# TensorE's order in an adaLN transformer block: a plan of time in place of a credit

## The chip, the cores and the metric

The kernel runs on one core of a Trainium2 chip. The metric is the device time of one execution in microseconds (us), as a median over several executions. Five engines matter: TensorE (PE, with its weight loads PEld), VectorE (DVE), ScalarE (ACT), GpSimd (POOL) and SyncE (SP), which here only issues DMAs.

## The reference

One transformer block in float32 over 2048 tokens of width 576. Six modulation vectors come from `c`; an attention with 32 heads of width 18 and a feed-forward layer of width 4608 with SiLU stand in two residual branches.

```python
mod = (silu(c) @ w_mod).reshape(...)            # sa, ca, ga, sb, cb, gb
h = layernorm(x) * (1 + ca) + sa
q, k, v = split(h @ wqkv)                       # 32 heads x 18
p = softmax(q @ k.T * 18 ** -0.5)
x = x + ga * ((p @ v) @ wo)
h = layernorm(x) * (1 + cb) + sb
x = x + gb * (silu(h @ w1) @ w2)
```

## The kernel before

Each float32 product that needs accuracy is made of three passes over split operands (high, low) in the fast `fp32r` type: 14 passes cover the 576 inputs of a projection (`PASS`). The product of probabilities and values is plain float32.

A prologue makes the layer norm, V for all tokens and the first Q and K. Then the attention goes over four blocks of 512 queries (`NQB`), in each over eight quads of four heads (`NQUAD`), 32 quads in all. In each quad two streams run, shifted by `LEAD` = 38 pairs of slots:

- `slot_a`: scores with queries on the partitions (`psa`), for a maximum over keys on VectorE (`mx`). `max_a` and `max_b` turn the maxima into extra rows of Q (transpose `pst`, then four DMAs on SP).
- `slot_b`: scores with keys on the partitions (`psb`); ScalarE takes the exponential into a tile `pt`. `pt` has 7 buffers (`PB`).

The two use opposite halves of TensorE's rows (54 and 56 of 64), so a `psa` and a `psb` matmul run side by side: one score pair, counted as one slot (`now`). A quad has 64 slots. `pv` adds a key tile's values into `psv`: four float32 matmuls side by side in four column groups. 16 key tiles make a quad's values; ScalarE copies them (`ov`), and `out_b` transposes them (`pso`) for division by the sums.

Between slots TensorE does filler work from a list (`Filler`): in block 0 the remaining Q and K projections (`qk_pair`), in blocks 1 to 3 the output projection (`proj`) and the feed-forward layer (`mlp1`, `mlp2`) of the block before. What is left of block 3's comes after the attention, alone, as the tail. A filler product has two PSUM banks (`Pair`), one for each half of the rows; a step is two matmuls side by side, and in the middle of a pair the halves change banks, which waits for a turn on ScalarE (`nop`). PSUM's eight banks are rings: `psb` 2, `psv` 1, and in block 0 `psF` 2 and `psA` 3; from the end of block 0 `psF` 3 and `psA` 2. The rings `psF` (fillers, `ps`, `psqk`, `psT`) and `psA` (`psa`, `pst`, `pso`) are what the change reckons with.

TensorE runs its instructions in the order in which the program writes them; those of the other engines are put in order by the build. The order of TensorE is set by the main loop: a slot, then values when due (`PVD` = 4 slots behind a second key tile, always two tiles: `PVN`), then filler steps as far as a credit allows, which grows by the same amount each slot and is charged for values (`PVC`). Nothing in it asks whether a bank is free.

Of the kernel before, what the change touches and what calls it, by code (L numbers as in the profile page):

```python
# [60 lines left out]
PVN = 2  # L61
DEBT = 1500.0
# [14 lines left out]
IDLE = 1  # L77
PVX = 300.0
PVC = 550.0
# [9 lines left out]

class Filler:  # L90


    def __init__(self):
# [7 lines left out]
    def add(self, cost, fn=None, name=None, fresh=False):  # L101

        self.items.append((cost, fn, name, fresh))
        self.total += cost

    def pace(self, slots):
        self.rate = (self.total - self.done) / max(slots, 1)
        self.credit = 0.0

    def _one(self):  # L110
        cost, fn, _, _ = self.items[self.pos]
        self.pos += 1
        self.done += cost
        if fn is not None:
            fn()
        return cost

    def step(self, extra=0.0, force=False):
        self.credit += self.rate + extra
        given = 0.0  # L120
        while self.pos < len(self.items) and not (given > 0 and self.items[self.pos][3]) and (self.credit > 0 or (force and given <= 0 and self.credit > -DEBT)):
            cost = self._one()
            self.credit -= cost
            given += cost
        return given > 0

    def until(self, name):
        last = max(i for i, it in enumerate(self.items) if it[2] and name in it[2])
        while self.pos <= last:
            self.credit -= self._one()  # L130

    def flush(self):
        while self.pos < len(self.items):
            self._one()
# [3 lines left out]
def tile_adaln_block(ctx: ExitStack, tc: tile.TileContext, x, wqkv, wo, w1, w2, c, wfirst, wcol, out):  # L138
# [70 lines left out]
    PASS = list(passes())  # L209

    class Pair:
# [6 lines left out]
        def __init__(self, ps, ops, n, halves):  # L218
            self.ps, self.ops, self.n, self.halves = ps, ops, n, halves

        def step(self, s):
# [5 lines left out]
            for h in (1, 0) if late else (0, 1):  # L227
# [4 lines left out]
                if h == 1 and s == self.n - 1:  # L232
                    self.turn = nc.scalar.nop()
                    tc.add_manual_dep(self.turn.ins, done.ins.name, SYNC, reason="the last of the first halves")
                elif h == 1 and s == self.n:
# [30 lines left out]
    def mod_piece(m, t):  # L266
# [5 lines left out]
        nc.scalar.activation((ga if m == 0 else gb)[:, t * P:t * P + n], ps[:, :n], AF.Copy)  # L272

# [22 lines left out]
    def qk_pair(which, m, ns, w, part):  # L296
# [8 lines left out]
        if part == NG - 1:  # L305
            for g in range(2):
                qk_out(which, m, ns[g], qk_ps[0].ps[g])

# [133 lines left out]
    state = {"now": 0, "k": 0, "tail": False, "tail2": False}  # L442
# [5 lines left out]
    fill = Filler()  # L448
    qk_w = {}

    def add_qk(steps):
# [5 lines left out]
        for i, (which, m, pairs) in enumerate(steps):  # L457
            for ns in pairs:
                names = [("qkx"[which], m, n) for n in ns]
                for p in range(NG):  # L460
                    fill.add(MMC * len(GR[p]), lambda i=i, which=which, m=m, ns=ns, p=p: qk_pair(which, m, ns, qk_w[i], p), name=names, fresh=p == NG // 2)
# [63 lines left out]
    later = []  # L525

    def slot_a(s, j):
# [11 lines left out]
        nc.vector.tensor_reduce(t["mx"][:, 2 * j + hp, stt, kc:kc + 1], ps, axis=AX.X, op=ALU.max)  # L539
        if j == 1 and s % 32 == 31:  # L540
            now = 2 * s + 1
            later.append((now, lambda: max_a(t)))
            later.append((now + MB, lambda: max_b(t)))

    def max_a(t):
# [5 lines left out]
        t["ms"] = ms  # L551

    def max_b(t):
# [3 lines left out]
        nc.vector.tensor_copy(mt, ps[:32, :P])  # L557
        for i in range(4):
# [3 lines left out]
    def slot_b(s, j):  # L562
# [3 lines left out]
        if j == 0:  # L566
            if w == 0:
                if i == 0:
                    fill.pace(NQUAD * 64 - END0)
                t["P"] = {}  # L570
            if w == 16 and i + 1 < NQ:
                load_v(i + 1)
            t["P"][kt, hp] = att.tile([P, 2, QB], F32, tag="p", name="pt", bufs=PB)
# [6 lines left out]
        if hp == 1 and j == 1 and kt % PVN == PVN - 1:  # L580
            later.append((state["now"] + PVD, lambda: pv(i, t, kt - PVN + 1, PVN)))

    def pv(i, t, k0, n):
        state["pv"] = True
        fill.credit -= PVC * n
        if k0 == 0:
            t["ps"] = psV.tile([P, QB], F32, tag="v", name="psv2")
        for kt in range(k0, k0 + n):
# [4 lines left out]
        if k0 + n == NKT:  # L593
            ov = att.tile([P, QB], F32, name="ov", bufs=1)
            nc.scalar.activation(ov, t["ps"], AF.Copy)
            later.append((state["now"] + 2, lambda: out_b(i, ov)))

    def out_b(i, ov):
# [11 lines left out]
        for s4 in range(NST):  # L610
            nc.vector.tensor_mul(o[b][:, s4, 72 * qd:72 * qd + 72].rearrange("p (h c) -> p h c", h=4), psr[:, s4, :, :DH],
                                 rec[:, s4, :, None].to_broadcast([P, 4, DH]))
        del quads[i]
# [5 lines left out]
    def open_mlp():  # L619
# [6 lines left out]
        mp["p"] = ctx.enter_context(tc.tile_pool(name="mlp", bufs=1, side="right"))  # L626

# [33 lines left out]
    def post(b):  # L661
# [3 lines left out]
        fl.__init__()  # L665
        ob = o[b]
        c = ready[b]
        last = state["tail"] = b == NQB - 1

        def o_T(kt):  # L670
# [6 lines left out]
            hi = c["th"][:, kt, :]  # L677
            nc.scalar.activation(hi, ps, AF.Copy)
# [5 lines left out]
        def proj(j, part):  # L684
# [8 lines left out]
            if part == len(GP) - 1:  # L693
                for g in range(2):
                    add_x1(j, g, c["pp"].ps[g])

# [9 lines left out]
        def ln_a(j):  # L706
            mv = pool.tile([P, 1, 2], F32, name="mv2", bufs=4)
            ln_stats(pool, c["x1"][j], mv[:, 0, :])
            c["ln", j] = mv, ln_rstd(pool, mv, 1)
# [5 lines left out]
        def h_T(kt):  # L715
# [3 lines left out]
            ps = bank("psT", psF)  # L719
            for j in range(NST):  # L720
# [7 lines left out]
        for kt in range(KT):  # L728
            fl.add(600, lambda kt=kt: o_T(kt))
        if b == 0:  # L730
            fl.add(LP0)
        for j in range(NST):
            rest(4 if j < 3 else 0)
            for part in range(len(GP)):
                fl.add(MMH * 7, lambda j=j, part=part: proj(j, part), fresh=part == 2)
                if part == 2 and j:
# [4 lines left out]
        rest(3)  # L741
# [27 lines left out]
        def mlp1(i, part):  # L769
# [11 lines left out]
            if not state["tail"]:  # L781
# [3 lines left out]
                nc.vector.tensor_copy(us[1], c["p1"].ps[1])  # L785
            for g_ in range(2):
# [8 lines left out]
        def mlp2(i0, j, part):  # L795
# [10 lines left out]
            for hf in range(2):  # L806
                add_x1(j, hf, c["p2"].ps[hf])
            if i0 + CH == NFT:
                nc.sync.dma_start(out[b * QB + j * P:b * QB + (j + 1) * P, :], c["x1"][j])

        if not EARLY:
            for kt in range(KT):
                fl.add(1100, lambda kt=kt: h_T(kt), name=["h_T"])
# [3 lines left out]
        if EARLY:  # L817
            if b == 0:
                fl.add(LP)
            for kt in range(KT):  # L820
                fl.add(1100, lambda kt=kt: h_T(kt), name=["h_T"])

        def add_mlp1(i, w2n=()):

            for part in range(NG):
                fl.add(MMC * len(GR[part]), lambda part=part: mlp1(i, part), fresh=part == NG // 2)
# [7 lines left out]
        def add_mlp2(i0, add):  # L834
            for j in range(NST):
                for part in range(len(G2)):
                    add(MMH * len(G2[part]), lambda j=j, part=part: mlp2(i0, j, part), None, part == 2)
# [12 lines left out]
        else:  # L850
            fl.add(0, lambda: prefetch(b + 1))
            add_mlp2(NFT - CH, lambda *a: left.append(a))
            fl.pace(NQUAD * 64 - END)

    def run_later(now):
        nonlocal later
        due = [e for e in later if e[0] <= now]
        later = [e for e in later if e[0] > now]
        for e in due:
            e[1]()  # L860
# [9 lines left out]

    fill.rate = V_RATE
    fill.step(WARM)
    fill.credit = 0.0
    idle = 0
    for now in range(2 * (total + LEAD + 8)):
        state["now"] = now
        state["pv"] = False
        sa, j = divmod(now, 2)
# [3 lines left out]
        if sa < LEAD:  # L882

            if j == 0:
                slot_a(sa, 0)
                slot_a(sa, 1)
        elif sa < total:
            slot_a(sa, j)
        if now >= ON0 and now % ONS == 0 and (now - ON0) // ONS < 2 * NKB:
            ones_rows(*divmod((now - ON0) // ONS, 2))  # L890
        if 0 <= sa - LEAD < total:
            slot_b(sa - LEAD, j)
        run_later(now)
        if sa < LEAD:
            fill.step()
        else:
            p0 = state["pv"]
            if p0:
                fill.credit += fill.rate + PVC / 4
                if fill.credit > PVX:  # L900
                    fill.step(-fill.rate)
                idle = 0
            elif fill.step(PVC / 4, idle >= IDLE):
# [53 lines left out]
```

## Time and profile before

| | |
|---|---|
| median of 3 runs | 2694.21 us (2691.33 to 2695.09) |
| the profiled execution | 2698.32 us, span 2696.5 us |
| mean granted TensorE clock | 0.972 |
| PE / DVE / ACT / POOL busy | 93% / 66% / 55% / 22% |
| scores' maxima on DVE (L539) | 2048 x 687 ns |
| exponentials on ACT (L579) | 2048 x 597 ns |

The span is the time from the first to the last instruction of the profiled execution. An engine's busy share is over the whole span. In a row of waits stand the engine and line that waited, who ended it, the sum in us, the count and the longest. In a timeline row stand the start, the length, engine, line, operation, tiles out<-in, shapes and count; in brackets the idle time before it and who ended that.

### The profile page before, as it was taken

The numbers are of one execution on the slowest core, as the hardware profiler recorded it, in microseconds if no ns is written. First come the engines' busy times: TensorE is split into PE (matmuls) and PEld (weight loads), VectorE is DVE, ScalarE is ACT, GpSimd is POOL, SyncE is SP. The second block draws the span as 40 slices with busy tenths as digits, with TensorE's granted clock in tenths as the row PEclk, the third lists the DMA queues.
The fourth block names the chain that finished last, engine by engine and source line by source line (L and its number), as shares of the span: only waits on it lengthen the run. The fifth ranks groups of instructions, "written<-read, shape, count | busy, mean of one in ns | idle before, by whom it ended". The sixth has DMA issues, their size and how long they took to land.

```text
span 2696.5 us, 51333 instructions
## 1 busy us (share of the span) xinstructions
PE 2505.7 (93%) x20248; PEld 1657.0 (61%) x20248; DVE 1771.5 (66%) x3097; ACT 1483.4 (55%) x2696; POOL 600.6 (22%) x827
## 2 busy tenths in 40 slices
PE   6969999998899999999899999999899999999999
PEld 5845444442456666666566666666566666658998
DVE  8367787776776777776776777666777676514333
ACT  2205676665565666666566666665666666661211
POOL 4200000002356556563211111111211111111000
PEclk8979999997999999999999999999999999999999
DMA  7452323324245545554433333333433333324653
GB/s 241 155 191 83 112 82 98 101 76 160 90 157 173 172 154 170 180 164 149 146 107 119 137 126 119 137 115 108 163 128 120 137 118 105 112 95 175 220 193 129
DMA packets 155042, 372.03 MB, mean 138 GB/s; under 512 B 17498, under 2 KB 50682, under 8 KB 154802
## 3 DMA queue, kind: packets, MB, share of 16 engines
q1 hardware_dynamic: 154658, 368.45, 40.2%
q8 instruction: 161, 2.64, 0.4%
q14 instruction: 79, 0.65, 0.1%
q10 hardware_dynamic: 144, 0.29, 0.1%
HBM read 282.35 MB, written 85.80 MB: 137 GB/s over the span
## 4 chain that ended last, share of the span: by engine, by line
PE 75%; DVE 15%; ACT 4%; issue 3%; DMA 2%; POOL 1%; SPq 0%; ACTq 0%; DVEq 0%; POOLq 0%
PE ps L231 22%; PE psv L591 17%; PE psa L537 12%; PE ps L225 9%; DVE mx L539 8%; PE psb L577 7%; PE psqk L231 3%; DVE etmp L789 2%; ACT pt L579 2%; PE psv L391 2%; PE psp L231 1%; DVE x L700 1%; ACT etmp L788 1%; ACT etmp L784 1%; PE psp L225 1%
## 5 line engine op out<-in xcount | busy, mean ns | idle before, releaser
L539 DVE TENSOR_REDUCE mx<-psa 128x1 f32<-128x512 f32 x2048 | 1345.0, 687 | 571.9 <-PE psb L577 286.9
L579 ACT ACTIVATE pt<-psb 128x512 f32<-128x512 f32 x2048 | 1171.9, 597 | 739.1 <-PE psb L577 416.3
L577 PE MATMUL psb<-qt,kt 56*128 56x512 f32 x2048 | 846.2, 441 | 17.0 <-ACT pt L579 13.3
L537 PE MATMUL psa<-kt,qt 54*128 54x512 f32 x2048 | 797.5, 427 | 53.8 <-DVE mx L539 33.1
L537 PEld LDWEIGHTS psa<-kt,qt 54*128 54x128 f32 x2048 | 365.8, 189 | 375.4 <-issue 164.7
L591 PE MATMUL psv<-pt,vt 128*32 128x512 f32 x4096 | 516.9, 624 | 0.0
L231 PE MATMUL ps<-w2t,g 64*128 64x288 f32 x4992 | 449.8, 300 | 23.0 <-DVE x L700 13.1
L231 PEld LDWEIGHTS ps<-w2t,g 64*128 64x128 f32 x4992 | 394.0, 187 | 75.3 <-DVE x L700 33.4
L231 PE MATMUL ps<-hh,w1t 64*128 64x512 f32 x2160 | 412.6, 402 | 11.3 <-ACT etmp L784 8.8
L577 PEld LDWEIGHTS psb<-qt,kt 56*128 56x128 f32 x2048 | 362.1, 187 | 84.0 <-ACT pt L579 65.5
L231 PEld LDWEIGHTS ps<-hh,w1t 64*128 64x128 f32 x2160 | 229.0, 186 | 72.5 <-ACT etmp L784 13.1
L591 PEld LDWEIGHTS psv<-pt,vt 128*32 128x32 f32 x4096 | 109.9, 112 | 244.7 <-issue 244.2
L792 POOL TENSOR_TENSOR g<-etmp,g 128x512 fp32r<-128x512 f32 x108 | 141.0, 1321 | 492.0 <-ACT g L791 381.7
L704 POOL TENSOR_TENSOR x<-x,gt 128x288 f32<-128x288 f32 x116 | 93.3, 804 | 487.0 <-ACT gt L703 463.7
L231 PE MATMUL ps<-hl,w1t 64*128 64x512 f32 x864 | 191.3, 393 | 0.0
L700 DVE TENSOR_TENSOR x<-ps,x 128x288 f32<-128x288 f32 x184 | 83.9, 456 | 113.6 <-PE ps L225 75.4
L225 PE MATMUL ps<-w2t,g 128*128 128x288 f32 x960 | 132.2, 297 | 3.3 <-ACT g L791 1.7
L225 PEld LDWEIGHTS ps<-w2t,g 128*128 128x128 f32 x960 | 129.9, 190 | 5.2 <-ACT g L791 2.2
L231 PE MATMUL psqk<-hTh,wqh 64*128 64x512 f32 x300 | 98.5, 433 | 22.8 <-DVE qkhl L312 22.2
L231 PEld LDWEIGHTS ps<-hl,w1t 64*128 64x128 f32 x864 | 98.5, 186 | 15.3 <-issue 0.3
L280 POOL TENSOR_TENSOR wql<-raw,wqh 128x640 fp32r<-128x640 f32 x13 | 20.7, 1591 | 389.5 <-ACT wqh L279 188.3
L225 PE MATMUL ps<-hh,w1t 128*128 128x512 f32 x360 | 106.9, 390 | 0.5 <-DVE hh L199 0.5
(127 smaller groups left out, 2125.4 us busy)
## 6 DMA issues: line engine op xcount, KB each, us to landing
w1t<-w1s SPq DMA_DIRECT2D x108, 640.0 KB
w2t<-w2s SPq DMA_DIRECT2D x108, 576.0 KB
kt<-kscr SPq DMA_DIRECT2D x512, 108.0 KB
w1s<-w1t SPq DMA_DIRECT2D x36, 640.0 KB
w2s<-w2t SPq DMA_DIRECT2D x36, 576.0 KB
vt<-vscr SPq DMA_DIRECT2D x32, 608.0 KB
qt<-qscr SPq DMA_DIRECT2D x128, 108.0 KB
raw<-in_w SPq DMA_DIRECT2D x72, 160.0 KB
```

Of the source, the lines that this page charges most:

```text
L225: mm(self.ps[late], lhsT=lhsT, rhs=rhs, start=(i == 0), stop=(i == self.n - 1))
L231: done = mm(self.ps[g], lhsT=lhsT[rows], rhs=rhs[rows], start=(s == 0), stop=(s == 2 * self.n - 1))
L391: mm(ps[:, :HH], lhsT=act[:, kt, ts], rhs=wv[kt][:, b, hf * HH:(hf + 1) * HH], start=(i == 0), stop=(i == 13))
L537: mm(ps, lhsT=t["q"][64 * j:64 * j + 54, hp, stt * P:(stt + 1) * P], rhs=t["k", kc, hp][64 * j:64 * j + 54, :], start=True, stop=True)
L539: nc.vector.tensor_reduce(t["mx"][:, 2 * j + hp, stt, kc:kc + 1], ps, axis=AX.X, op=ALU.max)
L577: mm(ps, lhsT=t["k", kt // 4, hp][64 * e:64 * e + 56, kt % 4 * P:(kt % 4 + 1) * P], rhs=t["q"][64 * e:64 * e + 56, hp, :], start=True, sto ...
L579: nc.scalar.activation(t["P"][kt, hp][:, e, :], ps, AF.Exp, scale=SCALE)
L591: mm(t["ps"][32 * h:32 * h + 32, :], lhsT=t["v"][:, c0:c0 + 32], rhs=t["P"][kt, h // 2][:, h % 2, :], start=(kt == 0), stop=(kt == NKT - 1 ...
L700: nc.vector.tensor_add(c["x1"][j][:, hs], ps, c["x1"][j][:, hs])
L704: nc.gpsimd.tensor_add(c["x1"][j][:, hs], c["x1"][j][:, hs], t)
L789: nc.vector.scalar_tensor_tensor(t, t, 1.0, u, op0=ALU.add, op1=ALU.mult)
L792: (nc.vector if last else nc.gpsimd).tensor_tensor(g[:, 1, :], t, f(g[:, 0, :]), op=ALU.subtract)
```

## The change

The credit is replaced by `Plan`, which keeps a clock `t` of TensorE, a queue for ScalarE and VectorE with a price for each evacuation, and for each ring of banks the times at which its banks come free. While the program is written, the main loop asks it before each decision whether the next thing could start at once: a score pair needs a free `psa` and `psb` bank and a free `pt`; a filler pair two banks (`pair_need`), its middle the turn (`half_need`); values need their exponentials. It takes what is ready, steered by how far the slots stand ahead of the filler (`AHEAD`). Values go in runs of one to three key tiles as they are ready. Filler steps are cut finer (`G2`, `GP`). Nothing of it runs on the chip: only the order of the instructions changes. In the last block's tail the plan is off.

```diff
-PVN = 2
-DEBT = 1500.0
-G2 = [range(i, i + 6) for i in range(0, 24, 6)]
-GP = [range(i, i + 7) for i in range(0, 28, 7)]
+G2 = [range(i, i + 3) for i in range(0, 24, 3)]
+GP = [range(i, i + 2) for i in range(0, 28, 2)]
+TS, TV, TX, TL, TR = 231, 906, 290, 430, 60
+TMAX, TEXP = 690, 600
+AHEAD = 12
+LOADED = 900
+STAND = 0
+class Plan:
...
+    def op(self, eng, ready, dur, done=None):
+        self.n += 1
+        heapq.heappush(self.queue[eng], (ready, self.n, dur, done))
...
+    def when(self, name, n=1):
+        size, rel = self.rings[name]
+        ts = [0]
+        for i in range(len(rel), len(rel) + n):
+            if i >= size:
+                if i - size >= len(rel) or rel[i - size] is None:
+                    return None
+                ts.append(rel[i - size])
+        return max(ts)
...
+    def is_ready(self, when):
+        return self.off or when is not None and when <= self.t
...
 class Filler:
-    def step(self, extra=0.0, force=False):
-        self.credit += self.rate + extra
...
+    def target(self):
+        return self.span[0] + self.span[1] * self.done / max(self.total, 1.0)
...
+    def ready(self):
+        need = self.items[self.pos][3]
+        return need is None or self.plan.is_ready(need())
...
+    def pair_need():
+        return plan.when("f", 2)
...
-        if hp == 1 and j == 1 and kt % PVN == PVN - 1:
-            later.append((state["now"] + PVD, lambda: pv(i, t, kt - PVN + 1, PVN)))
+        plan.op("A", plan.t + TL - TS + 30, TEXP, done)
+        if hp == 1 and j == 1:
+            pend.append((i, t, kt, at))
...
+    def run_pv(n):
+        i, t, kt, _ = pend[0]
+        plan.t += TX + TV * n
+        pv(i, t, kt, n)
+        del pend[:n]
...
-    for now in range(2 * (total + LEAD + 8)):
...
+        n = kts_ready()
+        room = state["p"] + (now % 2 == 0) <= PB
+        scores = more and room and plan.is_ready(plan.when("b")) and (now // 2 >= total or plan.is_ready(plan.when("a")))
+        busy = work and fill.ready()
+        if n >= 3 or n and more and not room and (ahead < 0 or not busy):
+            do = "v"
+        elif not mp:
+            if scores and ahead < AHEAD:
+                do = "s"
+            elif n and plan.backlog("V") >= LOADED * n:
+                do = "v"
+            elif busy and ahead > -AHEAD:
+                do = "f"
...
+        elif busy and ahead >= 0:
+            do = "f"
+        elif n >= 2 and not busy:
+            do = "v"
+        elif scores and ahead < AHEAD:
+            do = "s"
+        elif busy and ahead > -AHEAD:
+            do = "f"
+        elif n >= 2 or n and stood >= STAND:
+            do = "v"
```

(`mp` is empty in block 0.) Three places show how the order of TensorE moves. In the rows `psa` and `psb` together are a score pair, `psv` values (`x4` is one key tile), `psqk` a step of a Q or K projection, `ps<-w2t,g` half a step of the second layer, `pso` the out transposes.

TensorE in block 0, quad 3, before: around a run of values.

```order
L231 MATMUL psqk<-hTh,wqh 128x512 x2
L231 MATMUL psqk<-hTh,wql 128x512 x2
L537 MATMUL psa<-kt_1243,qt 128x512
L577 MATMUL psb<-qt,kt_1248 128x512
L591 MATMUL psv_3971<-pt,vt_1250 32x512 x8
L537 MATMUL psa<-kt_1244,qt 128x512
L577 MATMUL psb<-qt,kt_1247 128x512
L537 MATMUL psa<-kt_1244,qt 128x512
L577 MATMUL psb<-qt,kt_1247 128x512
L537 MATMUL psa<-kt_1244,qt 128x512
L577 MATMUL psb<-qt,kt_1248 128x512
```

The same quad after:

```order
L655 MATMUL psa<-kt_1243,qt 128x512
L697 MATMUL psb<-qt,kt_1247 128x512
L655 MATMUL psa<-kt_1243,qt 128x512
L697 MATMUL psb<-qt,kt_1247 128x512
L734 MATMUL psv_3980<-pt,vt_1250 32x512 x4
L655 MATMUL psa<-kt_1243,qt 128x512
L697 MATMUL psb<-qt,kt_1248 128x512
L655 MATMUL psa<-kt_1243,qt 128x512
L697 MATMUL psb<-qt,kt_1248 128x512
L344 MATMUL psqk<-hTh,wqh 128x512 x2
L344 MATMUL psqk<-hTh,wql 128x512 x2
```

Two key tiles in one run became one tile every four score pairs, and three pairs in a row became two.

TensorE in block 2, quad 18, before: where one pair of the second layer ends and the next begins.

```order
L231 MATMUL ps_19194<-w2t,g 128x288
L231 MATMUL ps_19195<-w2t,g 128x288
L537 MATMUL psa<-kt_1247,qt 128x512
L577 MATMUL psb<-qt,kt_1237 128x512
L231 MATMUL ps_19306<-w2t,g 128x288
L231 MATMUL ps_19307<-w2t,g 128x288
```

After:

```order
L344 MATMUL ps_19208<-w2t,g 128x288
L344 MATMUL ps_19209<-w2t,g 128x288
L734 MATMUL psv_18877<-pt,vt_1250 32x512 x4
L655 MATMUL psa<-kt_1247,qt 128x512
L697 MATMUL psb<-qt,kt_1238 128x512
L655 MATMUL psa<-kt_1247,qt 128x512
L697 MATMUL psb<-qt,kt_1238 128x512
L344 MATMUL ps_19327<-w2t,g 128x288
L344 MATMUL ps_19328<-w2t,g 128x288
```

Between the two pairs there now stand a key tile of values and two score pairs instead of one score pair.

TensorE at the out transposes of quad 19, before and then after:

```order
L537 MATMUL psa<-kt_1237,qt 128x512
L577 MATMUL psb<-qt,kt_1241 128x512
L602 MATMUL pso<-ident,ov 128x128 x4
L231 MATMUL ps_19703<-hl,w1t 128x512
L231 MATMUL ps_19704<-hl,w1t 128x512
```

```order
L344 MATMUL ps_20761<-w2t,g 128x288
L344 MATMUL ps_20762<-w2t,g 128x288
L747 MATMUL pso<-ident,ov 128x128 x4
L734 MATMUL psv_20806<-pt,vt_1250 32x512 x8
L655 MATMUL psa<-kt_1245,qt 128x512
L697 MATMUL psb<-qt,kt_1236 128x512
```

They moved from behind a score pair, whose maximum frees the bank they need, to behind filler steps.

More of the change, by code (lines that the diff above doesn't have):

```diff
@@ L852, in post @@
             add_mlp2(NFT - CH, lambda *a: left.append(a))
[L853 to L860, printed above, removed]
+            fl.pace(state["now"], NQUAD * 64 - END)
     total = NQ * 32
@@ L881, in tile_adaln_block @@
             prefetch(0)
[L882 to L891, printed above, removed]
-            slot_b(sa - LEAD, j)
[L893 to L903, printed above, removed]
-                idle = 0
-            else:
-                idle += 1
+        state["now"] = now
```

254 lines of the change are left out of this document (209 added, 45 removed).

## The prediction

> **What bounds the kernel now.** I read the page first, then the span cut into blocks, then the places where TensorE waits, then single moments.
>
> ```profile
> span 2696.5 us, 51333 instructions
> PE 2505.7 (93%) x20248; PEld 1657.0 (61%) x20248; DVE 1771.5 (66%) x3097; ACT 1483.4 (55%) x2696; POOL 600.6 (22%) x827
> PE 75%; DVE 15%; ACT 4%; issue 3%; DMA 2%; POOL 1%; SPq 0%; ACTq 0%; DVEq 0%; POOLq 0%
> ```
>
> TensorE carries 75% of the chain that ended last, VectorE 15%. But 93% busy is not 93% at pace, since ends are modelled. So I price TensorE's work from start to start and look for what is left over. The stretches are cut at the copy of a quad's values (L595); columns are length, PE, PEld, DVE, ACT, POOL busy, granted clock, DMA share, GB/s.
>
> ```profile
> 272.50:608.20 335.70, 316.57 (x2044) 161.15 (x2044) 258.26 (x464) 227.81 (x423) 7.73 (x5) 0.97 0.30 94
> 608.20:677.10 68.90, 59.82 (x263) 18.88 (x265) 43.66 (x74) 37.74 (x65) 19.14 (x30) 0.73 0.48 155
> 677.10:1257.60 580.50, 545.02 (x4882) 350.99 (x4883) 417.14 (x697) 359.30 (x651) 323.33 (x464) 0.98 0.48 157
> 1257.60:1841.20 583.60, 553.89 (x5090) 363.15 (x5092) 411.30 (x704) 361.74 (x661) 92.68 (x110) 0.99 0.37 128
> 1841.20:2418.00 576.80, 546.16 (x5003) 355.62 (x5003) 358.25 (x620) 358.38 (x656) 92.80 (x110) 0.99 0.34 120
> ```
>
> These are quads 1 to 6 of block 0, its quad 7, and blocks 1, 2, 3 (580.5 + 583.6 + 576.8 = 1740.9 us). What lies ahead of 272.5 and behind 2418.0 keeps its order nearly. No engine but PE is over 77% in any of them.
>
> Paces, from one stretch of block 2:
>
> ```profile
> 1502.64 0.39 PE L537 MATMUL psa<-kt,qt 54*128 54x512 f32 x1
> ...
> 1505.92 0.40 PE L577 MATMUL psb<-qt,kt 56*128 56x512 f32 x1
> 1506.24 1.92 PE L591 MATMUL psv<-pt,vt 128*32 128x512 f32 x16
> 1506.70 0.13 PEld L591 LDWEIGHTS psv<-pt,vt 128*32 128x32 f32 x4 [0.30 <-issue]
> 1507.13 0.13 PEld L591 LDWEIGHTS psv<-pt,vt 128*32 128x32 f32 x4 [0.30 <-issue]
> 1508.10 0.50 PE L537 MATMUL psa<-kt,qt 54*128 54x512 f32 x1
> 1508.44 0.63 PE L231 MATMUL ps<-hh,w1t 64*128 64x512 f32 x4
> 1508.63 0.69 DVE L539 TENSOR_REDUCE mx<-psa 128x1 f32<-128x512 f32 x1 [1.60 <-PE psb L577]
> 1508.67 0.60 ACT L579 ACTIVATE pt<-psb 128x512 f32<-128x512 f32 x1 [1.69 <-PE psb L577]
> ...
> 1510.82 1.09 PE L231 MATMUL ps<-w2t,g 64*128 64x288 f32 x12
> 1511.62 0.40 PE L577 MATMUL psb<-qt,kt 56*128 56x512 f32 x1
> ```
>
> From 1502.64 to 1505.92 stand 14 units (a score pair or a step of two 512-column halves): 3.28 / 14 = 0.234 us each. Six steps of 288 columns take 1511.62 - 1510.82 = 0.80, so 0.133. A run of two key tiles of values goes by groups 0.43 apart, two to a tile, so 0.86 a tile. Around it: entry 0.32 instead of 0.234 (+0.09), 1508.10 - 1506.24 = 1.86 instead of 1.72 (+0.14), and the next unit 0.34 instead of 0.234 (+0.11). So each run, however long, costs 0.34 us beside its tiles. During it VectorE idles 1.60 and ScalarE 1.69 us.
>
> **Ledger of blocks 1 to 3**, by the counts in the order before: 1454 score pairs, 76 lone score halves and 1504 steps at 0.234 = 710.0; 2832 steps at 0.133 = 376.7; 384 value tiles at 0.86 = 330.2; 192 runs at 0.34 = 65.3; some 50 for transposes, which both orders share (an estimate). Sum 1532. So 1740.9 - 1532 = 209 us are waits and lost pace. Where they are, over these blocks:
>
> ```profile
> PE psa L537 <- DVE mx L539: 26.1, 47, 1.4
> PE ps L231 <- ACT etmp L784: 18.5, 39, 0.9
> PE ps L231 <- DVE x L700: 15.3, 62, 0.4
> PE pso L602 <- DVE mx L539: 13.7, 21, 1.3
> PE psb L577 <- DMA qt<-mt: 3.3, 1, 3.3
> PEld psa L537 <- DVE mx L539: 101.6, 165, 1.7
> PEld ps L231 <- DVE x L700: 42.2, 80, 0.8
> PEld ps L231 <- ACT etmp L784: 28.8, 33, 1.2
> PEld ps L231 <- ACTq L233: 22.4, 87, 0.5
> PEld pso L602 <- ACT pt L579: 19.8, 20, 1.7
> ```
>
> All but the one on a DMA are waits for a bank: a score's (psa), a filler pair's (ps; the ACTq rows are the turn between its halves), the out transposes' (pso). The PE rows are lower bounds, since a matmul's modelled end (0.40) lies past the next start (0.234); the PEld rows are upper ones. Filler pairs: between 33.8 and 93.4, taken at 85, near the upper end, because a held weight load holds its matmul. Scores: 26.1 to 101.6, taken at 60, the middle, because loads run ahead of scores. Out transposes and the maxima's: 13.7 to 33.5, taken at 23. The other 41 is lost pace, half clock included.
>
> **The change, part by part.** Both orders hold the same 18,190 matmuls; DVE, ACT, POOL and the DMAs do the same work. Only order moves.
>
> *Shorter runs of values.* The order before has 256 runs, all of two tiles. After there are 455: 128 in block 0, 327 in blocks 1 to 3. That is 135 more there, x 0.34 = +46 us of TensorE time, with nothing beside it to hide it. In block 0 it is 72 more, 24 us, laid where PE waits anyhow, so in its cycle below. The Trainium skill (TensorEngine Tiling (Array Packing), Key Properties) says that a change of tiling mode drains TensorE, which speaks against this part; this trace agrees with a cost, 0.34 us, and by the rule alone 199 runs would be 68 us lost.
>
> *Filler pairs.* Before, 59 of 72 second-layer pairs that follow one another start less than 1 us of TensorE work behind the last (median: one score pair, 0.23), while the evacuation takes:
>
> ```profile
> L700 DVE TENSOR_TENSOR x<-ps,x 128x288 f32<-128x288 f32 x104 | 47.2, 454 | 36.9 <-PE ps L231 21.2 <-PE psb L577 9.6
> L784 ACT ACTIVATE etmp<-ps 128x512 f32<-128x512 f32 x53 | 31.6, 595 | 9.7 <-PE ps L231 9.6
> ```
>
> Three banks serve pairs of two, so the second bank is always one just left. After, 5 of 72 start so early; the median stands 1.66 us behind, a value run and score pairs between, and the half-turns likewise. 0.454 or 0.595 plus some 0.5 until the result is there (1508.10 to 1508.63) fits in 1.66 even behind one maximum of 0.69. So 85 falls to 8: -77. What is late next is the maximum behind a crowded VectorE, below.
>
> *Scores.* Adjacent score pairs fall from 286 to 211, three in a row from 18 to 4. With two psa banks and 0.69 + 0.5 from score to free bank, the third in a row always waits; spaced ones wait when VectorE is behind with additions and copies. It is 72% busy in block 1, so some stay: 60 falls to 23, -37. Both ends: 0 and -60.
>
> *Out transposes.* 22 of 24 stood right behind a score and waited for its maximum; now 21 of 24 stand behind filler steps: 23 to 6, -17. The maxima's transpose and the four SP transfers behind it (L560) may come two slots later (a slot is one score pair); at least seven slots of 1740.9 / 1530 = 1.14 us stay before the first exponential needs them, some 8 us, which hide them. If that cover failed, the price is a wait like the one of 3.3 us on `qt<-mt` above, at most once a quad.
>
> *Block 0.* Here a score waits for ScalarE and its two banks:
>
> ```profile
> PEld psb L577 <- ACT pt L579: 51.1, 136, 1.1
> 419.86 0.49 PE L537 MATMUL psa<-kt,qt 54*128 54x512 f32 x1
> 426.53 0.49 PE L537 MATMUL psa<-kt,qt 54*128 54x512 f32 x1
> ```
>
> From behind one run of two to behind the next (eight score pairs) 6.67 us pass. After, a cycle of four pairs reads S S steps S S run: by the rows above the third pair can start 0.57 + 0.60 behind the first, the fourth 0.60 later, and the run with its pair takes 0.234 + 0.86 + 0.34 = 1.43, so 1.17 + 0.60 + 1.43 = 3.20, or 6.40 for eight. That is -0.27 x 8 cycles x 6 quads = -13; if ScalarE is never late, VectorE's four maxima with their side work (258.26 busy of 335.70) are the floor, -77 at most; 0 if drift eats it. I take -18, near the worked cycle. Quad 7 runs at a granted clock of 0.73, which costs up to 0.27 x 68.9 = 18.6; shorter gaps should give back half, -9. The Trainium skill (TensorE: Matmul & The Clock Gate, Part 1) says the clock halves after an idle window of about 3.4 us; by it all 18.6 would come back if no such window stays, and the trace agrees only so far that the low clock stands where PE has least work. 30 filler steps moved into quad 0: 30 x 0.234 = 7, half hidden, +3.
>
> **Sum.** -77 - 37 - 17 + 46 - 18 - 9 + 3 = -109. The profiled execution took 2698.3, 4.1 over the median of 2694.2: 2698.3 - 109 = 2589, less 4, 2585.
>
> **Rivals.** (A) *The switches cost more than the waits, slower.* 85 us over 170 pair starts and as many half-turns is 0.25 a place, less than the 0.34 that now covers it. If filler waits are only the 33.8 of the PE rows, scores keep theirs, and in block 0 PE becomes the bound (+24): -34 - 17 + 46 + 24 = +19, 2713; up to +68. It decides where less than 46 of the 209 go. Against it: starts of less than 1 us are nearly gone. 0.13. (B) *VectorE takes the waits over*: maxima stand behind the additions, and a third of 168 goes: -56 + 46 - 24 = -34, 2660. Speaks for it: 15% of the chain. 0.15. (C) *All 209 go*: -209 + 46 - 24 = -187, 2507. 0.15. (D) *Nothing comes of it*, since the engines' own queues are ordered apart from TensorE's and stand behind each other anew: within 0.2%, about what a measurement here can tell. 0.05.
>
> **How the numbers follow.** The forecast has 0.52 (own range 2540 to 2630). Faster: 0.52 + 0.15 + 0.15 = 0.82; same 0.05; slower 0.13. From 2500 (C, and a little of its tail left out) to 2690 (B and D in, A out) stands 0.82.
>
> **What would show it.** Right: filler waits on etmp and x near nothing; the out transposes' wait for maxima gone; blocks 1 to 3 at 535 to 555 us each; about 450 runs of values with 0.34 around each; VectorE's idle behind a run about 0.8, not 1.60. Wrong: psa waits on mx over 80 us in PE rows (B), blocks over 580 with filler waits gone (A), block 0 unmoved with ScalarE still the releaser.

## The result and the profile after

The changed kernel takes 2561.6 us (median of 4 runs, 2560.43 to 2563.05) against 2694.65 for the kernel before on the same chip: a ratio of 0.9505 [0.9489, 0.9522], 133 us less. 2585 was forecast, so it gained more than it was to, by some 23 us. The profiled execution took 2563.05 us.

The page of the changed kernel: span, busy times, and who carries the chain that ended last.

```profile
span 2561.2 us, 51319 instructions
PE 2448.4 (96%) x20248; PEld 1630.9 (64%) x20248; DVE 1773.2 (69%) x3097; ACT 1489.4 (58%) x2696; POOL 603.9 (24%) x827
PE 85%; DVE 7%; DMA 3%; ACT 2%; POOL 2%; issue 1%; SPq 0%; ACTq 0%; DVEq 0%
```

Against the same lines of before: as many matmuls on the same tiles, TensorE at 85% of the chain (was 75%), VectorE at 7% (was 15%). So less of the chain runs over VectorE; which waits of TensorE went is seen below.

The span of the changed kernel cut at the same events as before: quad 0 and what is ahead of it, quads 1 to 6 of block 0, quad 7, then blocks 1, 2 and 3, and the tail (start:end, length, busy time and count of PE, PEld, DVE, ACT and POOL, granted clock, DMA share, GB/s).

```profile
0.00:288.80 288.80, 222.68 (x1392) 165.70 (x1394) 175.52 (x342) 84.90 (x154) 54.91 (x75) 0.91 0.49 162
288.80:609.20 320.40, 314.73 (x1980) 148.12 (x1982) 258.75 (x460) 225.08 (x420) 7.77 (x5) 0.99 0.31 93
609.20:665.50 56.30, 46.22 (x269) 16.07 (x271) 42.95 (x74) 37.09 (x67) 19.14 (x30) 1.00 0.60 192
665.50:1217.70 552.20, 537.00 (x4914) 348.74 (x4914) 420.08 (x706) 366.52 (x662) 322.88 (x464) 0.99 0.51 167
1217.70:1746.90 529.20, 526.11 (x5018) 352.30 (x5020) 407.59 (x697) 359.07 (x652) 93.23 (x110) 1.00 0.40 135
1746.90:2284.30 537.40, 533.96 (x5037) 356.16 (x5039) 360.52 (x622) 362.90 (x659) 92.80 (x111) 1.00 0.39 132
2284.30:2561.20 276.90, 267.70 (x1648) 243.85 (x1648) 107.83 (x197) 53.80 (x88) 13.20 (x33) 1.00 0.51 179
```

| us | before | after | change | forecast |
|---|---|---|---|---|
| up to the end of quad 0 | 272.5 | 288.8 | +16.3 | +3 |
| quads 1 to 6 | 335.7 | 320.4 | -15.3 | -18 |
| quad 7 | 68.9 | 56.3 | -12.6 | -9 |
| block 1 | 580.5 | 552.2 | -28.3 | |
| block 2 | 583.6 | 529.2 | -54.4 | |
| block 3 | 576.8 | 537.4 | -39.4 | |
| blocks 1 to 3 | 1740.9 | 1618.8 | -122.1 | -85 |
| tail | 278.5 | 276.9 | -1.6 | 0 |

Two differences stand out: blocks 1 to 3 gained 37 us more than forecast, and the start lost 16.3 where 3 had been allowed. They partly cancel in the total.

TensorE's waits in blocks 1 to 3 of the changed kernel, the window 665.5 to 2284.3 (engine and line that waited, who ended it: sum in us, count, longest):

```profile
PE psa L655 <- DVE mx L657: 7.5, 15, 1.7
...
PE pso L747 <- ACT pt L699: 1.2, 1, 1.2
PE pso L747 <- DVE mx L657: 0.6, 1, 0.6
...
PEld psa L655 <- DVE mx L657: 105.6, 145, 1.9
...
PEld ps L344 <- ACTq L346: 7.3, 9, 0.8
...
PEld ps L344 <- DVE x L851: 1.7, 4, 0.8
```

The filler pairs' waits for their evacuations, 33.8 us in the PE rows and 93.4 in the PEld rows before, are gone but for some 9. So is the out transposes' wait for maxima (13.7, now 0.6). Scores' waits for their bank fell from 26.1 to 7.5 in the PE row, while the PEld row stayed where it was (101.6, now 105.6). What that row holds is seen in the timeline of weight loads, here in block 2:

```profile
1507.88 0.16 PEld L734 LDWEIGHTS psv<-pt,vt 128*32 128x32 f32 x8 [0.16 <-issue]
1508.88 0.18 PEld L655 LDWEIGHTS psa<-kt,qt 54*128 54x128 f32 x1 [0.84 <-DVE mx L657]
1508.88 0.29 PEld L697 LDWEIGHTS psb<-qt,kt 56*128 56x128 f32 x2
```

The first load behind a run of values stands idle 0.84 us (the median before and after) while the values are worked off, whatever releaser is named. That is no wait for a bank, and it lies in the 0.86 of a tile and the 0.34 of a run already. Of the 145 in the row after, some 100 with 85 us are of this kind; of the 165 before, 31 with 26. So I sum the idle ahead of every weight load of blocks 1 to 3 but the values' own, whatever its releaser, and leave out the first load behind a run of values. What remains is called held loads below; it is worked out from the timelines of blocks 1 to 3, where idle time of 0.15 us or more is told.

Values in block 0 of the changed kernel, from the timelines of VectorE and TensorE (start, length, work; in brackets the idle time before it):

```profile
421.04 2.48 DVE L657 TENSOR_REDUCE mx<-psa 128x1 f32<-128x512 f32 x4 [0.74 <-PE psa L655]
...
424.17 2.48 DVE L657 TENSOR_REDUCE mx<-psa 128x1 f32<-128x512 f32 x4 [0.65 <-PE psa L655]
...
427.31 2.48 DVE L657 TENSOR_REDUCE mx<-psa 128x1 f32<-128x512 f32 x4 [0.65 <-PE psa L655]
```

```profile
422.64 1.07 PE L734 MATMUL psv<-pt,vt 128*32 128x512 f32 x8
...
423.63 0.50 PE L655 MATMUL psa<-kt,qt 54*128 54x512 f32 x1
...
423.97 0.40 PE L655 MATMUL psa<-kt,qt 54*128 54x512 f32 x1
```

Four maxima come every 3.13 us (3.20 was worked out), and VectorE idles 0.65 behind a run (0.8 was). A run of one tile costs what a run of two does beside its tiles: from its start to the next score 0.99 = 0.86 + 0.13, and the unit behind that score takes 0.34 instead of 0.234. (The x8 counts matmul records, two to each of the four matmuls.)

### The profile page after: what moved, and what is told of

Read it like the earlier page. It is cut to its first block, busy times and chain, and to the rows that moved or that the text cites. A ratio compares the mean times of both kernels' runs of the same rounds, so it can differ in the third digit from the quotient of the medians.

```text
span 2561.2 us, 51319 instructions
## 1 busy us (share of the span) xinstructions
PE 2448.4 (96%) x20248; PEld 1630.9 (64%) x20248; DVE 1773.2 (69%) x3097; ACT 1489.4 (58%) x2696; POOL 603.9 (24%) x827
## 4 chain that ended last, share of the span: by engine, by line
PE 85%; DVE 7%; DMA 3%; ACT 2%; POOL 2%; issue 1%; SPq 0%; ACTq 0%; DVEq 0%
PE ps L344 26%; PE psv L734 19%; PE psa L655 14%; PE ps L338 9%; PE psb L697 9%; DVE mx L657 3%; PE psqk L344 3%; PE psv L508 2%; PE psp L344 2%; DMA kt<-kscr 1%; ACT pt L699 1%; PE pso L747 1%; PE psp L338 1%; DVE st L257 0%; DVE qkhl L429 0%
## 5 line engine op out<-in xcount | busy, mean ns | idle before, releaser
L697 PE MATMUL psb<-qt,kt 56*128 56x512 f32 x2048 | 825.9, 430 | 7.6 <-ACT pt L699 5.5
L655 PE MATMUL psa<-kt,qt 54*128 54x512 f32 x2048 | 803.3, 422 | 20.3 <-DVE mx L657 16.3
L734 PE MATMUL psv<-pt,vt 128*32 128x512 f32 x4096 | 543.2, 605 | 0.0
L344 PEld LDWEIGHTS ps<-w2t,g 64*128 64x128 f32 x4992 | 403.8, 186 | 70.4 <-issue 36.6
L697 PEld LDWEIGHTS psb<-qt,kt 56*128 56x128 f32 x2048 | 355.3, 184 | 68.5 <-ACT pt L699 58.1
L344 PE MATMUL ps<-hh,w1t 64*128 64x512 f32 x2160 | 381.3, 395 | 0.7 <-POOL hh L287 0.6
L344 PEld LDWEIGHTS ps<-hh,w1t 64*128 64x128 f32 x2160 | 218.0, 186 | 58.1 <-issue 16.8
L734 PEld LDWEIGHTS psv<-pt,vt 128*32 128x32 f32 x4096 | 90.9, 108 | 154.7 <-issue 148.0
L344 PE MATMUL ps<-hl,w1t 64*128 64x512 f32 x864 | 182.6, 393 | 1.3 <-POOL hl L285 1.3
L344 PE MATMUL psqk<-hTh,wqh 64*128 64x512 f32 x300 | 84.7, 428 | 35.5 <-DVE qkhl L429 34.8
L943 ACT ACTIVATE eq<-ps 128x512 f32<-128x512 f32 x36 | 21.5, 599 | 146.3 <-PE ps L338 146.3
```

What stands on the lines that cost most here:

```text
L344: done = mm(self.ps[g], lhsT=lhsT[rows], rhs=rhs[rows], start=(s == 0), stop=(s == 2 * self.n - 1))
L655: mm(ps, lhsT=t["q"][64 * j:64 * j + 54, hp, stt * P:(stt + 1) * P], rhs=t["k", kc, hp][64 * j:64 * j + 54, :], start=True, stop=True)
L697: mm(ps, lhsT=t["k", kt // 4, hp][64 * e:64 * e + 56, kt % 4 * P:(kt % 4 + 1) * P], rhs=t["q"][64 * e:64 * e + 56, hp, :], start=True, sto ...
L734: mm(t["ps"][32 * h:32 * h + 32, :], lhsT=t["v"][:, c0:c0 + 32], rhs=t["P"][kt, h // 2][:, h % 2, :], start=(kt == 0), stop=(kt == NKT - 1 ...
```

## The experiments

Three things had to be explained: what of the gain is the plan's asking for free banks (**banks**), what is the shorter runs of values (**short runs**), and why the start lost. The forecast had held banks to be nearly everything, and short runs a cost of 46 us. All ratios are to the kernel before, run beside each on the same chip.

### The start: a smaller head for quad 0

The list of projections has a credit of `WARM` ns ahead of the first slot. Before, `step` stopped after 14 of its steps, in the middle of the first pair, where the halves change banks (a step marked `fresh`); the changed `step` has no such stop, and 52 steps run ahead.

```diff
-WARM = 12000.0
+WARM = 3200.0
```

> The changed kernel with 14 instead of 52 filler steps ahead of the first score (WARM 3200 instead of 12000). Theory of the late start: quad 0 ended 16.3 us later because 38 steps (38 x 0.234 = 8.9 us, with their own bank waits) went ahead of the first maxima, in a block that VectorE and ScalarE bound. It expects quad 0 to end 9 to 14 us sooner and some of it to be kept: 2549 to 2555 us. Rival: the steps are only moved, and TensorE pays for them later: 2559 to 2563 us.

Measured: 2539.53 us, 0.9423 [0.941, 0.9435], some 22 us less than the changed kernel and better than both ranges. Quad 0 ends at 264.0 us instead of 288.8. What had gone wrong there is in two views of the changed kernel, the waits between 140 and 230 us and ScalarE's timeline:

```profile
PE psqk L344 <- DVE qkhl L429: 32.1, 8, 15.5
...
ACT wqh L395 <- DMA raw<-in_wqkv: 26.7, 1, 26.7
```

```profile
154.38 0.60 ACT L428 ACTIVATE qkhl<-psqk 128x512 fp32r<-128x512 f32 x1 [8.08 <-DMA kscr<-qkhl]
...
181.65 0.74 ACT L395 ACTIVATE wqh<-raw 128x640 fp32r<-128x640 f32 x1 [26.68 <-DMA raw<-in_wqkv]
182.29 1.07 ACT L428 ACTIVATE qkhl<-psqk 128x512 fp32r<-128x512 f32 x2
```

ScalarE's cast of the next weights (L395) waits 26.68 us for their DMA, and the copies that empty the projections' banks (L428) stand behind it in ScalarE's queue. TensorE, 38 steps further than before, has both banks full and waits up to 15.5 us. With the smaller head the first of these rows reads:

```profile
PE psqk L344 <- DVE qkhl L429: 9.9, 6, 3.8
```

That is 22.2 us less of this wait, and quad 0 ends 24.8 us sooner.

### Banks asked for, but runs of two

```diff
-        n = kts_ready()
+        n = 2 if kts_ready() >= 2 else 0
```

> The changed kernel with values always in runs of two key tiles (256 runs instead of 455), all else planned. Theory of the banks (the gain comes from laying values and score pairs where TensorE would wait for a bank; a run's switch is a loss of 0.34 us): 199 x 0.34 = 68 us less work on TensorE, of which 46 in blocks 1 to 3, against covers that are missing at a part of the pair starts (40 of 72 second-layer starts stand within 1 us again), 25 to 45 us: 2540 to 2562 us. Theory of the short runs (the gain comes from VectorE and ScalarE idling less behind a short run): most of the 122 us of blocks 1 to 3 come back, 2640 us or more.

Measured: 2613.48 us, 0.9696 [0.9683, 0.971], with 256 runs as before. Both missed: it lies 52 us above the changed kernel and 81 below the one before. The two parts of its span, quads 1 to 7 of block 0 and blocks 1 to 3:

```profile
290.70:700.50 409.80, 382.92 (x2247) 177.62 (x2249) 299.76 (x534) 265.54 (x485) 26.86 (x35) 0.93 0.31 99
700.50:2334.70 1634.20, 1590.67 (x14967) 1085.36 (x14969) 1183.40 (x2024) 1084.25 (x1971) 504.66 (x684) 0.99 0.43 144
```

Block 0 is no better than before (404.6); blocks 1 to 3 keep 107 of their 122 us.

### The old credit with runs of one

In the kernel before:

```diff
-PVN = 2
+PVN = 1
```

> The kernel before with values in runs of one tile (512 instead of 256), its credit order else unchanged. Theory of the banks: 256 x 0.34 = 87 us more work on TensorE and no wait covered on purpose; some fall under waits that were there anyhow: slower than before, 2720 to 2780 us. Theory of the short runs: faster than before by 60 us or more, 2635 us or less.

Measured: 2659.87 us, 0.9863 [0.9847, 0.9878], 1.4% less than before with 512 runs, twice as many. Both ranges missed again.

```profile
266.60:651.10 384.50, 369.20 (x2321) 170.41 (x2323) 305.00 (x537) 264.40 (x488) 26.93 (x35) 0.97 0.35 110
651.10:2382.30 1731.20, 1662.43 (x14969) 1028.76 (x14971) 1200.24 (x2021) 1094.63 (x1967) 510.49 (x684) 1.00 0.40 136
```

So neither theory held alone. Before, after and these two make a square (profiled executions, us):

| order, runs of values | block 0, quads 1 to 7 | blocks 1 to 3 |
|---|---|---|
| credit, twos (before) | 404.6 | 1740.9 |
| credit, ones | 384.5 | 1731.2 |
| plan, twos | 409.8 | 1634.2 |
| plan, mostly ones (after) | 376.7 | 1618.8 |

The new theory read off it: in block 0 the gain is the length of the runs (-20 under the credit, -33 under the plan), and the plan by itself gives little (+5 and -8). In blocks 1 to 3 it is the plan (-107 and -112), and shorter runs no more than repay what they cost (-10 and -15).

### The plan, not asking for the fillers' banks

```diff
-need={0: pair_need, len(G2) // 2: half_need}.get(part)
+need=None
```

(the same for the projections and the first layer)

> The changed kernel whose filler steps no longer ask for their banks or the turn; scores and values are still planned. 343 runs of values (230 of one tile, 57 of two, 56 of three). Theory of the banks: the waits of filler pairs come back, 75 to 100 us, less 112 runs x 0.34 = 38: 2595 to 2625 us, with PEld rows on x and etmp at 70 us or more. Theory of the short runs: most runs stay short, no more than 15 us are lost: 2550 to 2577 us.

Measured: 2677.3 us, 0.9931 [0.9918, 0.9945], far beyond both ranges. Block 0 stays (379.3); blocks 1 to 3 take 1738.2, nearly as before:

```profile
669.60:2407.80 1738.20, 1645.19 (x14993) 1087.12 (x14993) 1190.71 (x2027) 1090.12 (x1975) 508.86 (x685) 1.00 0.41 136
```

The waits in that window are back where the forecast had seen them:

```profile
PE ps L344 <- DVE x L851: 35.3, 86, 1.0
...
PE ps L344 <- ACT etmp L937: 20.1, 42, 0.9
...
PEld ps L344 <- DVE x L851: 67.5, 95, 1.2
PEld ps L344 <- ACTq L346: 40.3, 133, 0.9
PEld ps L344 <- ACT etmp L937: 31.2, 36, 1.3
```

Held loads of filler pairs are 167.7 us, where the changed kernel has 9.1. The order also has 112 runs of values fewer, worth 38 us at 0.34, so the loss of 119.4 stands for some 157 of waits, and the fillers' own 158.6 more account for it. (The plan's clock does not count these waits here, so scores and values are planned on a clock that is behind; the held loads of `psa` rose by only 10.) Asking before a filler pair carries blocks 1 to 3. The finer filler steps (`G2`, `GP`) are not the gain: this order has them too.

### Runs of two only behind block 0

The kernel with the small head, and in blocks 1 to 3 a second tile waited for:

```diff
         n = kts_ready()
+        if mp:
+            n = min(n, 1) if pend and pend[0][2] % 2 else 2 if n >= 2 else 0
```

> The kernel with the early start (WARM 3200) and runs of two key tiles in blocks 1 to 3 alone; block 0 keeps its runs of one. New theory (length matters by place: in block 0, where VectorE and ScalarE bind, short runs are worth some 33 us; in blocks 1 to 3 the 0.34 us of each further run and the score waits that it saves nearly cancel): block 0 as with the early start (378 us for quads 1 to 7), blocks 1 to 3 together 10 to 20 us longer than its 1617: 2549 to 2560 us. Rival (all of what runs of two lost, 52 us, comes back with them wherever they are): 2575 us or more. A gain would say that the switches are the greater cost.

Measured: 2563.49 us, 0.9506 [0.9485, 0.9528], against 0.9423 with the small head alone. The new theory's range was missed by a little, the other's by more. Blocks 1 to 3 lost 22.7 us (1639.5 against 1616.8), 135 runs fewer (-46 at 0.34) and 69.7 us more of held loads (134.0 against 64.3), which makes +24. Quad 7, where the edit sets in early, lost 7.3 more.

### The turn in the middle of a pair not asked for

```diff
-need={0: pair_need, len(G2) // 2: half_need}.get(part)
+need={0: pair_need}.get(part)
```

> The changed kernel whose filler pairs still ask for two free banks at their start, but not for the turn in their middle. 360 runs of values instead of 455. Theory of the banks with the start as the costly place: a turn waits some 0.25 us at 170 places, 42 us, against 95 runs x 0.34 = 32 us saved: 2562 to 2585 us. If the turn were as costly as the start (half of the 119 us that blocks 1 to 3 lost without both): 2610 us or more. Theory that the switches are the greater cost: 2550 us or less.

Measured: 2557.34 us, 0.9491 [0.9473, 0.951], between the ranges and not to be told from the changed kernel. The turn's wait is back in blocks 1 to 3:

```profile
PEld ps L344 <- ACTq L346: 44.1, 138, 0.6
```

It was 7.3, and held loads in all rose from 65.6 to 112.8. But there are 95 runs of values fewer in these blocks, 32 us at 0.34, and the blocks took only 4.4 more: what covers the turn costs about what the turn did in this order (the last run below says otherwise for another).

### Transposes at their due time

The plan also lets the out transposes and the maxima's wait until what they need is there. Here they stand at their due time:

```diff
             if cost:
-                plan.wait(when)
-                plan.wait(lambda: plan.when("a"))
                 plan.t += cost
...
-        run_later()
+        run_later(True)
```

> The changed kernel in which the transposes of the maxima and of the values go out when due, whether or not their bank and input are ready by the plan. Theory of the banks: their waits (23 us by the ledger of before, of which 17 were forecast to go) come back: 2572 to 2585 us. Rival (they are covered by TensorE's distance to their inputs anyhow): 2558 to 2566 us.

Measured: 2574.86 us, 0.9554 [0.9537, 0.9571], as expected; blocks 1 to 3 took 15.4 us more. The forecast's -17 for this step is about right. The waits in these blocks:

```profile
PE pso L747 <- DVE mx L657: 8.5, 17, 0.9
PE pst L675 <- DVE mx L657: 7.1, 10, 1.5
```

### How far the slots may run ahead

With the small head:

```diff
-AHEAD = 12
+AHEAD = 24
```

> The kernel with the early start and twice the leash between slots and filler (AHEAD 24 instead of 12), tried for a better time. If what is left (12 us in block 2, 9 in block 3, 36 in block 1 over the paced work) comes from steps that had to go by the leash although something else was ready: 2525 to 2535 us. If it comes from the start of block 1, where no filler is there yet: within 5 us of the early start, 2535 to 2545 us.

Measured: 2533.43 us, 0.9399 [0.9383, 0.9416], the lowest of all, though its interval just overlaps that of the small head alone. The total is in the first range. By the one profiled execution of each, quads 1 to 6 took 4.2 us less than with the small head alone and block 1 4.5 less, blocks 2 and 3 did not move, and quad 7 took 3.8 more. Then twice as far again:

```diff
-AHEAD = 12
+AHEAD = 48
```

> Early start with AHEAD 48. If AHEAD 24 gained 6 us because the leash forbade ready work, and block 1's start is what is left: 2522 to 2534 us. If more leash only moves filler out of quad 7, where it runs out (60.4 us with 24, 56.6 with 12): 2534 to 2545 us.

Measured: 2541.87 us, 0.9424 [0.9412, 0.9437], no better than 12 and in the second range. But the loss is in quads 1 to 6 (325.3 against 317.4), not in quad 7, which took 2.9 less than with 24.

Last, the lowest so far without the turn:

> The best so far (early start, AHEAD 24) whose filler pairs ask for their banks at the start but not for the turn in the middle: 343 runs of values instead of 451. If the turn's cover costs about what the turn's wait does, as the run without the turn said (4 us faster than the changed kernel): 2524 to 2534 us. If runs of two and three bring back score waits as in blocks 1 to 3 with runs of two (15 to 23 us): 2540 to 2555 us.

(The small head, `AHEAD` 24 and the turn not asked for.) Measured: 2564.05 us, 0.9514 [0.9501, 0.9527], worse than either range. Blocks 1 to 3 took 1648.8 us, 35.8 more than with the turn asked for: 107 runs fewer (-36), and held loads up by 69 (135.6 against 66.7), 45 of it fillers and some 20 `psa`. In the first order without the turn the fillers' had risen as much (+42) and those of `psa` by 11.5. Why scores suffer more in this order, and so whether asking for the turn pays, stays open.

### One account for all of them

Blocks 1 to 3 of nine kernels: runs of values there, held loads by kind in us, their length, and what is left of the length without 0.34 a run and without held loads. Of the scores the first kind has `psa` alone; `psb` stands with the transposes (`psT`, `pso`, `pst`), with 9.2 us before and 8.4 after.

| | runs | `psa` | filler pairs | `psb`, transposes | sum | length | left |
|---|---|---|---|---|---|---|---|
| before | 192 | 86.5 | 106.4 | 53.0 | 246.0 | 1740.9 | 1429.6 |
| credit, ones | 384 | 52.4 | 93.6 | 34.2 | 180.1 | 1731.2 | 1420.5 |
| after | 327 | 24.5 | 9.1 | 32.0 | 65.6 | 1618.8 | 1442.1 |
| plan, twos | 192 | 62.7 | 28.7 | 39.4 | 130.9 | 1634.2 | 1438.0 |
| fillers not asking | 215 | 34.7 | 167.7 | 22.3 | 224.7 | 1738.2 | 1440.4 |
| small head, late twos | 192 | 61.1 | 28.6 | 44.4 | 134.0 | 1639.5 | 1440.2 |
| turn not asked for | 232 | 36.0 | 50.9 | 25.9 | 112.8 | 1623.2 | 1431.5 |
| transposes when due | 323 | 24.6 | 13.1 | 49.4 | 87.1 | 1634.2 | 1437.3 |
| small head, `AHEAD` 24, no turn | 217 | 45.3 | 53.8 | 36.5 | 135.6 | 1648.8 | 1439.4 |

The lengths differ by 122 us, what is left by 22. So two things, the number of runs at 0.34 and the held loads, account for nearly all that these orders do to blocks 1 to 3. (What is left lies 25 to 46 us below the forecast's price of the work without runs, 1532 - 65 = 1467. So held loads say somewhat too much; that part of them hides behind matmuls that still run is likely, but not shown.)

## Why the prediction was right, and where not

**Blocks 1 to 3, the mechanism.** Waits for banks were the loss, and a plan that asks before each pair takes them away: shown by the two orders with runs of two (1740.9 to 1634.2, -106.7 at the same 192 runs) and by its undoing (+119.4 where fillers don't ask). The wait rows that were to fall fell. Rival B fell with them: the scores' wait for maxima is 7.5 us in the PE row, where 80 were its mark. Rival A too, whose blocks would have been over 580, and D, which would have left the waits as they were. C came nearest after the forecast: 171 of its 209 went.

**Blocks 1 to 3, the size.** By the forecast's own prices, with the counts of the changed kernel: 1533 score pairs and lone halves and 1512 steps at 0.234, 2832 at 0.133, 384 tiles at 0.86, 327 runs at 0.34 and 50 make 1580.6. Of 1618.8 us 38 are left as waits and lost pace; it was 209. So 171 went where 131 were forecast, and the +46 for 135 more runs came as costed. The held loads say where:

| us | forecast | held loads, before to after |
|---|---|---|
| filler pairs | -77 | 106.4 to 9.1: -97 |
| scores (held loads: `psa`) | -37 | 86.5 to 24.5: -62 |
| transposes (held loads: with `psb`) | -17 | 53.0 to 32.0: -21 |
| sum | -131 | -180 (the ledger: -171) |

The mis-sized steps are "60 falls to 23" first, then "85 falls to 8", and with them "The other 41 is lost pace", of which most was waits. (By held loads, which say somewhat too much.) The scores ended where they were forecast to, at 24.5, but began at 86.5: 60 was taken as the middle of a PE row and a PEld row, and the PEld row leaves out loads whose wait bears another releaser's name and counts the values' own time in. The fillers' 85 lies below their 106.4 for a like reason: the rows cited leave out the waits under other names and those of the output projection (`psp`).

What shorter runs give back was left out. With runs of two the plan took 107 us; going on to mostly ones cost 46 and still gained 15, since held loads fell by 65: `psa` 38, fillers 20, the rest 7. The forecast booked the further runs in these blocks as a cost with no return. It had seen the return in its rows (VectorE idle 1.60 and ScalarE 1.69 us behind each run of two) and used it for block 0 alone.

**Out transposes.** -17 forecast; when this part is undone, +15.4 in blocks 1 to 3, where the held loads of `pso` and `pst` go up by 22.6 (13.8 to 36.4) and the whole column by 17.4. Right. The maxima's four transfers on SP came in time, too: the largest wait of a score on `qt<-mt` is 1.3 us in blocks 1 to 3, where it was 3.3.

**Block 0.** -18 and -9 were forecast, -15.3 and -12.6 came. The cycle after is as worked out (3.13 against 3.20), and the run length moves the block, under either order. But the shorter cycle is the smaller part of the gain. Here are the quads that ran wholly at full clock, three before and then two and three after:

```profile
332.60:495.60 163.00, 155.64 (x1025) 79.69 (x1025) 129.37 (x235) 114.43 (x214) 4.65 (x3) 1.00 0.32 97
288.80:397.80 109.00, 105.41 (x660) 48.68 (x662) 87.67 (x156) 76.53 (x143) 3.11 (x2) 1.00 0.33 101
452.30:609.20 156.90, 155.64 (x993) 74.39 (x995) 128.08 (x227) 111.24 (x208) 3.11 (x2) 1.00 0.28 88
```

That is 163.0 / 3 = 54.3 us a quad before and (109.0 + 156.9) / 5 = 53.2 after. So at one clock the change is worth about 1.1 us a quad, where 0.27 x 8 = 2.2 was forecast, and by this estimate some 8 of the 28 us of seven quads. The rest goes with the clock: length times clock is 404.6 x 0.93 = 376 us before, 384.5 x 0.97 = 373 with the old order and ones, 409.8 x 0.93 = 381 with the plan and twos, and 376.7 x 1.00 after. Why the clock stayed up is not shown, and that the sum for block 0 came out so near is in part luck.

**Quad 0.** "+3" came out as +16.3. This is the step that failed at the start. It counted the steps that moved and their cover, and not the queue they moved past: 52 steps ahead of the first slot instead of 14 reach weights that have not landed, and a cast that waits for them holds the copies behind it on ScalarE. That was in the trace of before, where the same cast waits 17.4 us for the same DMA, and it is shown by the small head: -24.8 us in quad 0.

**The total and smaller slips.** Blocks 1 to 3 gained 37 us more than forecast and the start lost 13 more. The two errors have opposite signs, and that 2585 lies within 24 us of 2561.6 is luck to that extent. Block 2 with 529.2 fell below the 535 to 555 that were to show the mechanism. Block 0 has 64 more runs of values, not 72 (before 64 and 192, after 128 and 327): 22 us, not 24, and rival A 2 us lower. The 33.5 for the transposes adds a PE row to a PEld row, where the other kinds take the PEld rows alone. And the 0.82 for 2500 to 2690 is C, the forecast and B; D, within 0.2% of 2694, lies outside it but for its edge.

## What to carry to other kernels

Where one engine's order is fixed, ask before each piece of work whether its bank is free, not only how much work is due: here that was worth 107 us of 1741, and 119 when it was taken away. Price a switch of mode together with the waits that a long run makes for the others: 135 further runs at 0.34 cost 46 us and saved 65 of held loads, 15 us in all. To size waits, count idle weight loads whatever their releaser, without those behind a long run of other work. And when work is drawn forward, follow its inputs to the queue where they are made, since one waiting cast held all of ScalarE's copies behind it for 26.7 us here.

## What the runs showed of the hardware

In quad 7 of the kernel before the granted clock halves without any long pause of TensorE. Three stretches of that quad, TensorE's timeline around its start, and TensorE's longest waits in the whole quad:

```profile
611.80:618.60 6.80, 6.76 (x26) 1.93 (x28) 3.39 (x5) 2.95 (x5) 0.00 (x0) 0.50 0.49 171
622.00:636.00 14.00, 13.12 (x54) 3.99 (x52) 7.29 (x12) 6.63 (x12) 10.51 (x17) 0.51 0.68 221
636.00:652.00 16.00, 12.98 (x76) 4.33 (x72) 12.04 (x19) 10.89 (x19) 5.58 (x9) 1.00 0.58 192
```

```profile
606.25 1.92 PE L591 MATMUL psv<-pt,vt 128*32 128x512 f32 x16
...
611.74 0.79 PE L537 MATMUL psa<-kt,qt 54*128 54x512 f32 x1
...
614.78 3.64 PE L591 MATMUL psv<-pt,vt 128*32 128x512 f32 x16
```

```profile
PE psa L537 <- DVE mx L539: 6.0, 19, 0.5
PE psa L537 <- DVE ot L611: 0.7, 1, 0.7
```

A run of values of the same size takes 3.64 us at the low clock instead of 1.92, and no wait in the quad is over 0.7 us. The changed kernel has a longer one in its quad 7, 0.9 us, and a full clock (1.00):

```profile
PE psa L655 <- DVE mx L657: 8.1, 15, 0.9
```

With runs of two brought back behind block 0 the clock fell again, to 0.84 in a quad 7 of 63.9 us:

```profile
583.90:647.80 63.90, 54.38 (x273) 18.01 (x275) 43.17 (x74) 37.73 (x66) 19.26 (x30) 0.84 0.54 174
```

The forecast had cited the Trainium skill (TensorE: Matmul & The Clock Gate, Part 1) on an idle window of some 3.4 us; no such window stands in quad 7 before, so that rule doesn't account for the low clock there. The same page of the Trainium skill (TensorE: Matmul & The Clock Gate, A second HAM failure mode: psum-queue depth-cycling) tells of a clock that swings when TensorE idles for short moments between groups often enough. The trace agrees so far that the clock fell with no wait over 0.7 us; that the short waits are the cause no run here shows. More idle time in all does not go with less clock: by length less PE busy, 56.30 - 46.22 = 10.1 us of idle after went with 1.00, 68.90 - 59.82 = 9.1 before with 0.73.

What differs is the length of the runs of values between the waits. The three orders with runs of two in quad 7 (in one of them all but two runs) have a clock of 0.73, 0.79 and 0.84 there; of the nine with runs of one, seven have 1.00 and one 0.94. But the ninth, the old credit with runs of one, has 0.86:

```profile
591.20:651.10 59.90, 51.29 (x279) 16.96 (x281) 43.83 (x75) 37.72 (x67) 19.20 (x30) 0.86 0.56 179
```

So the run length goes with the clock here, but it can't be all of it, and the cause stays open.
